# A spectral mixer's inverse table in two thirds, its load order, and the rings that its inverse tiles come from

## The chip, the cores and the metric

The kernel runs on one core of a Trainium2 chip. A core has a matrix engine (TensorE, "PE" in the profile, with its weight loads as "PEld"), VectorE ("DVE"), ScalarE ("ACT"), GpSimd ("POOL") and SyncE ("SP"), which here only issues DMAs. Work is passed between the engines by semaphores, and each engine runs its own instructions in order. PE writes to PSUM, eight banks of 2 KB in each of 128 partitions. The metric is the device time of one execution in microseconds. Before the change three runs gave 352.26, 358.77 and 361.63 us, with a median of 358.77.

## The reference

The forward pass mixes a sequence of 2048 rows with 448 features twice, once in the frequency domain and once by a two-layer network over the sequence; the outputs are the result and the gradients of everything.

```
h  = x + irfft2(rfft2(layernorm(x)) * (w_r + i w_i))        # 2048 x 448
u  = gelu(einsum("bsd,sf->bdf", layernorm(h), w1) + b1)      # f = 1792
out = h + transpose(einsum("bdf,fs->bds", u, w2) + b2)
grads of out with grad_out: x, w_r, w_i, w1, b1, w2, b2
```

## The kernel before

The Fourier transforms are matrix products with tables of cosines and sines that the host builds once (`_tables`). A transform over the 2048 rows is split 16 x 128, and the symmetries of a real input leave 225 of 448 columns; the sixteen parts of the row frequency are called j, and j and 16 − j are handled together.

The kernel is one long program. A scheduler puts the instructions of each engine in order, by the data they need; where the text says `issue_after`, an instruction is held behind another.

- **PSUM.** Eight banks in three rings: `m0` and `m1` with two buffers each (L215), and `sp` with four (L222). A tile that is asked for from a ring has to wait until the oldest buffer of that ring has been read.
- **Loads.** `nxt` (L237) chains the loads of SP in the written order. SP issues them in that order, and a load waits for the one eight places before it. Transposing loads go through `ld_t` (L232), others through `ld` (L226).
- **Forward transform.** `fft_rows` (L403) transforms rows in four quarters. `fft_cols` (L422) goes over eight pairs of j: two PSUM tiles from `sp`, a copy on ACT, sum and difference on VectorE (`gu`, `gv`, L484), then matmuls with the table `hf` into a tile of ring `m1` (L455), copied to `xs` by ACT.
- **Product.** `cmul` (L503) multiplies `xs` by the filter `w_t` in six groups of j, four VectorE operations each (L510 to L513), and writes over `w_t`.
- **Inverse transform.** `ifft_cols` (L519) takes the pairs of j in turn. `pair` asks for two tiles of PSUM (L522), one for each half of the partitions, and issues 16 matmuls of 64 x 128 (L534), whose moving operand is a row of the table `hi`. ACT copies the second tile (L551), and VectorE writes sum and difference of the two into `ab` (L553). The table `hi` holds for each j the pairs (cos, sin) and (−sin, cos), with the signs that the second half needs; it is 1 MB, `[128, 2, 16, 128]` in bf16 (L622).
- **Row steps.** Sixteen of them (L637): four matmuls with the table `di` (L578, L580), a copy on ACT, four with `kinv` (L587 to L590), then the residual and the layer norm. After every four steps ACT writes the normalized rows `hln` (L386).
- **Filling work.** `dg(j)` (L606) is 16 matmuls 448 wide of the gradient of the hidden layer (L610) with a transposed block of w2, `w2T`, into ring `m0`; after it the load of a further block is issued. dg(0) comes early; dg(1) to dg(3) and dg(4) to dg(13) are there to be put between the matmuls of the transforms. Behind them stand the first layer and the GELU (`gelu_in`, L683), the second layer (L752), and the gradient of the normalized rows (L811, with transposed blocks of w1, `w1T`).
- **Backward transform.** It uses the same functions with `twice=True`. There `fill(n)` hands out parts of the weight gradients (`gw2`, L259 for full chunks and L266 for tails), a counted number at each j; one part is half a block.

The loads around the change, and the three blocks behind them (L621 to L628 before):

```
load_w(w_t, nxt)
hi = consts.tile([P, 2, NJ, P], BF16, name="hi")
nxt(ld, hi[:], hnd["hi"].ap().rearrange("p (i j m) -> p i j m", i=2, j=NJ))
di0 = table([P, 4 * DF], "di0", "di")
kinv = table([P, 3, P], "kinv")
ident = table([P, P], "ident")
for j in range(1, 4):
    dg(j)
```

Of the kernel before, what the change touches and what calls it, by code (L numbers as in the profile page):

```python
# [11 lines left out]
BF16 = mybir.dt.bfloat16  # L12
F32 = mybir.dt.float32
ALU = mybir.AluOpType
# [3 lines left out]
P = 128  # L18
S = 2048
D = 448  # L20
DF = 225
# [4 lines left out]
NJ = 16  # L26
# [19 lines left out]
def _tables():  # L46
# [86 lines left out]
    p = 16 * (pp % 4) + pp // 4  # L133
# [15 lines left out]
            hf[64:, 3 + 2 * i + c] = sg * np.concatenate([np.sin(th), np.cos(th)], 1)  # L149
    tb["hf"] = _bf(hf.reshape(P, -1))  # L150

    hi = np.zeros((2, 64, 2, NJ, 2, 64))
    for c in range(2):
        for j in range(NJ):
            th = angle(j + 16 * c).T
            sg = -1.0 if c and j else 1.0
            hi[c, :, 0, j, 0], hi[c, :, 0, j, 1] = np.cos(th), sg * np.sin(th)
            hi[c, :, 1, j, 0], hi[c, :, 1, j, 1] = -np.sin(th), sg * np.cos(th)
    tb["hi"] = _bf(hi.reshape(P, -1))
    tb["ident"] = _bf(np.eye(P))  # L160
    return tb
# [3 lines left out]
def kernel(  # L165
# [29 lines left out]
    def slot(i, shape, name):  # L195
        return big.tile(shape, BF16, tag=f"s{i}", name=name)
# [18 lines left out]
    def ps_m(k, shape, dtype=F32):  # L215
        return psum.tile(shape, dtype, tag=f"m{k}", bufs=2, name=f"ps_m{k}")
# [5 lines left out]
    def ps_sp(shape, dtype=F32):  # L222
        return psum.tile(shape, dtype, tag="sp", bufs=4, name="ps_sp")
# [13 lines left out]
    def nxt(load, *args):  # L237
        if chain:
            with tc.issue_after(chain[-1].ins):
                chain.append(load(*args))  # L240
        else:
            chain.append(load(*args))
# [179 lines left out]
    def fft_cols(zt, dtab, dst, twice=False, fill=None):  # L422
        w = 226 if twice else DF

        def part(out, j, odd):
            lhs = [zt[:, 2 * odd + c, 2 * j:2 * j + 2, :] for c in range(2)]
            if twice:

                for c in range(2):
                    o = 113 * (2 * odd + c)  # L430
                    pe.matmul(out[:, 113 * c:113 * c + 113], lhsT=lhs[1 - c if odd else c], rhs=dtab[:, o:o + 113],
                              start=True, stop=True)
                return
            for c in range(2):
                o = DF * (2 * odd + c)
                pe.matmul(out, lhsT=lhs[c], rhs=dtab[:, o:o + DF], start=(c == 0), stop=(c == 1))

        def sums(nm):
            return k1([P, 2, w], nm)

        def in_order(t):
            return t.rearrange("p a (k c) -> p a c k", c=2) if twice else t

        def by_k(t):
            return t.rearrange("p a (c k) -> p a c k", c=2) if twice else t

        def out_j(j, u, v, behind):
            px = ps_sp([P, 2, DF]) if fill else ps_m(1, [P, 2, DF])
            if j:
                e = 1 + 2 * J_ORDER.index(j)  # L450
                lhs = [(b, g, hf[:, e + b, 64 * c:64 * c + 64]) for c in range(2) for b, g in ((1, v), (0, u))]
                for i, (b, g, m) in enumerate(lhs):

                    with tc.issue_after(behind[0].ins) if behind else nullcontext():
                        mm = pe.matmul(px[64 * b:64 * b + 64, i // 2, :], lhsT=m, rhs=g, start=True, stop=True)  # L455
                    behind = behind or [mm]
            else:
                for c in range(2):
                    for i, g in enumerate((u, v)):
                        pe.matmul(px[:, c, :], lhsT=hf[:, ((0, 2), (1, 0))[c][i], :], rhs=g,  # L460
                                  start=(i == 0), stop=(i == 1))
            ac.copy(out=dst[:, :, j * DF:(j + 1) * DF], in_=px[:])
            return behind

        def out_all(those):
            behind = []
            for args in those:
                behind = out_j(*args, behind)

        waiting = []
        for j in range(8):
            js = (j, 16 - j) if j else (0, 8)
            pt = [ps_sp([P, 2, w]) for odd in range(2)]
            for odd in range(2):
                for x, jj in enumerate(js):
                    part(pt[odd][:, x, :], jj, odd)
            first = 0 if j else 1
            gi = f2([P, 2, w], "gi")  # L480
            ac.copy(out=gi[:, first:, :], in_=pt[1][:, first:, :])  # L481
            u, v = sums("gu"), sums("gv")
            for g, op in ((u, ALU.subtract), (v, ALU.add)):
                ve.tensor_tensor(out=in_order(g[:, first:, :]), in0=by_k(pt[0][:, first:, :]),  # L484
                                 in1=by_k(gi[:, first:, :]), op=op)
            if not j:

                for g, ps in ((u, pt[0]), (v, pt[1])):
                    ac.copy(out=in_order(g[:, 0:1, :]), in_=by_k(ps[:, 0:1, :]))

            done = [(jj, u[:, x, 0:DF], v[:, 1 - x if j else x, 0:DF]) for x, jj in enumerate(js)]
            waiting += done
            if not fill or j:
                out_all(waiting[:-len(done)] if fill else waiting)
                waiting = done if fill else []
                if fill:
                    fill(2 if j in (1, 3, 6) else 1)
        out_all(waiting)


# [18 lines left out]
    def ifft_cols(ys, ab, twice=False, fill=None):  # L519
        def pair(js):  # L520

            pt = [ps_sp([P, 2, 2, P]) for b in range(2)]  # L522
            first = []
            for x, j in enumerate(js):
                for c in range(2):
                    for i in range(2):
                        for b in range(2):
                            d = slice(64 * b, 64 * b + 64)
                            jj = (16 - j) % 16 if b else j
                            k = jj * DF + (c if twice else 97 * c)  # L530
                            ks = slice(k, k + 2 * P - 1, 2) if twice else slice(k, k + P)

                            with tc.issue_after(first[-1].ins) if first else nullcontext():
                                mm = pe.matmul(pt[b][:, c, x, :], lhsT=ys[d, i, ks], rhs=hi[d, i, jj, :],  # L534
                                               start=(i == 0), stop=(i == 1))
                            first = first + [mm] if len(first) < 2 else first
            return pt

        def place(a, lo, hi_):
            return ab[:, a, :, :, lo:hi_, :].rearrange("p c h k l -> p k c h l")  # L540

        def view(t):
            return t.rearrange("p c x (k h l) -> p (x k) c h l", k=2, l=4)

        for j in (1, 2, 3, 4, 5, 6, 7, 0):
            pt = pair((j, 16 - j) if j else (8, 0))
            if fill and j:
                fill(1)
            n = 2 if j else 1
            t1 = f2([P, 2, 2, P], "t1")  # L550
            ac.copy(out=t1[:, :, 0:n, :], in_=pt[1][:, :, 0:n, :])  # L551
            for a, op in ((0, ALU.add), (1, ALU.subtract)):
                ve.tensor_tensor(out=place(a, 4 * j, 4 * j + 2 * n), in0=view(pt[0][:, :, 0:n, :]),  # L553
                                 in1=view(t1[:, :, 0:n, :]), op=op)
            if not j:
                for b in range(2):
                    ev(ab[:, :, :, :, 2 + b, :], view(pt[b][:, :, 1:2, :]), "av"[b])
# [48 lines left out]
    def dg(j):  # L606
        pg = ps_m(0, [P, D])
        with tc.issue_after(folded[min(j - 1, 3)][0].ins) if j else nullcontext():
            for t in range(NT):
                pe.matmul(pg[:], lhsT=w2T[j][:, t, :], rhs=go_nat[:, t, :], start=(t == 0), stop=(t == NT - 1))  # L610
        ev(du[:, j, 0:D], pg[:], "a")
        load_w2T()
# [6 lines left out]
        nxt(ld, hf[:, e0:e1], hf_d[:, e0:e1])  # L619
    w_t = slot(4, [P, 2, XW], "w_t")  # L620
    load_w(w_t, nxt)  # L621
    hi = consts.tile([P, 2, NJ, P], BF16, name="hi")  # L622
    nxt(ld, hi[:], hnd["hi"].ap().rearrange("p (i j m) -> p i j m", i=2, j=NJ))
    di0 = table([P, 4 * DF], "di0", "di")
    kinv = table([P, 3, P], "kinv")
    ident = table([P, P], "ident")
    for j in range(1, 4):
        dg(j)  # L628
    xs = slot(3, [P, 2, XW], "xs")
    fft_cols(zt, df1, xs)  # L630
    cmul(lambda r0, r1: (w_t[:, 0, r0 * DF:r1 * DF], w_t[:, 1, r0 * DF:r1 * DF]), xs, w_t, False)
    ab = slot(5, [P, 2, 2, NT, NR, 4], "ab")
    ifft_cols(w_t, ab)
    hn = x
# [197 lines left out]
            yield mm  # L832

    first = list(gw2(0, "aaaa"))
    fft_rows(dh, zt2, 3, "aava", first[-1], True)

    def blocks():
        for j in range(1, NFB):
# [6 lines left out]
    def fill(n):  # L845
        return [next(others) for i in range(n)]

    ds = slot(3, [P, 2, XW], "ds")
    fill(1)
    fft_cols(zt2, df0, ds, True, fill)  # L850
# [129 lines left out]
```

## Time and profile before

| | |
|---|---|
| three runs | 352.26, 358.77, 361.63 us |
| profiled execution | 351.85 us, its span 349.5 us |
| PE busy | 327.3 us (94%) |
| VectorE busy | 250.7 us (72%) |
| ACT busy | 207.6 us (59%) |
| granted PE clock | 1.00 |
| read from HBM, written | 32.41 MB, 28.93 MB |

The span is the time from the first to the last instruction; the profiled execution's own time has 2.35 us around it. Times in the rows of a timeline are in us from the span's start: first the start, then the duration, the engine, the line in the code, the operation, the output and the inputs. A bracket at the end of a row gives the idle time before it and what ended it. A matmul's duration runs from its first to its last element, so neighbouring matmuls overlap; the distance between two starts is what one costs. In a row of the windows stand the window, its length, then the busy time (and count) of PE, PEld, VectorE, ACT and POOL, the granted clock, the mean share of the DMA engines, and GB/s.

### The profile page before, as it was taken

How to read it: one execution, taken by the hardware profiler on the slowest of the kernel's cores; microseconds unless marked ns; L12 is line 12 of the kernel's file. 1: busy time of each engine (PE TensorE's matmuls, PEld its weight loads, DVE VectorE, ACT ScalarE, POOL GpSimd, SP SyncE). 2: the span in 40 equal slices, each digit the busy share in tenths (PEclk: the TensorE clock that was granted, in tenths of full speed). 3: DMA queues.
4: the chain of work that ended last, by engine and by line, in shares of the span. 5: the costliest groups of instructions: out<-in, count | busy, mean ns of one | idle time of the engine just before them, and what ended most of it. 6: DMA issues, size and time to landing. Idle time of an engine off the chain costs nothing.

```text
span 349.5 us, 6182 instructions
## 1 busy us (share of the span) xinstructions
PE 327.3 (94%) x2258; PEld 175.5 (50%) x2275; DVE 250.7 (72%) x586; ACT 207.6 (59%) x428; POOL 77.3 (22%) x133
## 2 busy tenths in 40 slices
PE   0799989999999999999999999999999999999995
PEld 0446544566655555555555555644544455454442
DVE  4894899777748988622225887864798797899932
ACT  3575643466759888200833444588885667777662
POOL 1000000011112110245511000001101124677960
PEclk9999999999999999999999999999999999999999
DMA  7999997999899999999999998999579437776485
GB/s 278 283 206 273 242 189 167 304 276 299 244 315 331 321 266 236 314 341 376 290 211 233 219 179 175 211 200 192 178 167 268 150 122 247 323 249 216 160 308 202
DMA packets 132878, 85.27 MB, mean 244 GB/s; under 512 B 92112, under 2 KB 124496, under 8 KB 132464
## 3 DMA queue, kind: packets, MB, share of 16 engines
q1 hardware_dynamic: 124400, 54.90, 68.2%
q0 software_dynamic: 8160, 29.85, 24.7%
q8 instruction: 18, 0.29, 0.4%
q14 instruction: 12, 0.10, 0.1%
q10 hardware_dynamic: 288, 0.13, 0.1%
HBM read 32.41 MB, written 28.93 MB: 175 GB/s over the span
## 4 chain that ended last, share of the span: by engine, by line
PE 62%; DVE 15%; DMA 9%; SPq 5%; issue 3%; ACT 3%; POOL 2%; DVEq 0%; ACTq 0%; POOLq 0%
PE ps_m L811 12%; PE ps_m L259 9%; PE ps_sp L752 6%; PE ps_m L752 6%; PE ps_m L683 6%; PE ps_sp L683 6%; PE ps_m L610 6%; DMA w_t<-in_A_w_i_dram 4%; DVE t_i L511 3%; DMA xs_b<-xs_d 3%; SPq L232 3%; DVE ab L553 2%; DVE t_r L510 2%; SPq L226 2%; DMA w2T<-in_B_w_dram 2%
## 5 line engine op out<-in xcount | busy, mean ns | idle before, releaser
L283 ACT CAST s<-ps_m 128x512 bf16<-128x512 f32 (+1 forms) x103 | 52.2, 573 | 15.9 <-PE ps_m L266 14.4
L610 PE MATMUL ps_m<-go_nat,w2T 128*128 128x448 bf16 x224 | 50.1, 359 | 1.6 <-DMA w2T<-in_B_w_dram 1.6
L811 PE MATMUL ps_m<-du,w1T 128*128 128x449 bf16 x224 | 43.4, 353 | 0.0
L259 PE MATMUL ps_m<-goT,g_t 128*128 128x512 bf16 x158 | 39.5, 380 | 0.7 <-issue 0.5
L229 POOL DMA_DIRECT2D out_dram<-s x28 | 15.2, 543 | 98.9 <-ACT s L283 77.7
L259 PE MATMUL ps_m<-du_t,hlnT 128*128 128x512 bf16 (+1 forms) x161 | 35.4, 352 | 1.2 <-ACT s L283 0.7
L752 PEld LDWEIGHTS <-w2c 128*128 128x128 bf16 x224 | 21.9, 98 | 20.5
L811 PEld LDWEIGHTS <-w1T 128*128 128x128 bf16 x224 | 21.7, 97 | 20.7
L683 PEld LDWEIGHTS <-w1c 128*128 128x128 bf16 x224 | 21.8, 98 | 20.5 <-issue 0.5
L610 PEld LDWEIGHTS <-w2T 128*128 128x128 bf16 x224 | 21.0, 99 | 18.6 <-DMA w2T<-in_B_w_dram 2.4
L752 PE MATMUL ps_sp<-gT,w2c 128*128 128x448 bf16 x112 | 30.3, 352 | 0.0
L752 PE MATMUL ps_m<-gT,w2c 128*128 128x448 bf16 x112 | 30.3, 352 | 0.0
L259 PEld LDWEIGHTS <-hlnT 128*128 128x128 bf16 x192 | 17.6, 98 | 21.1 <-issue 6.7
L757 DVE SCALAR_TENSOR_TENSOR h<-ps_m,b2col,hr 128x448 bf16<-128x448 f32 x8 | 5.1, 680 | 27.5 <-PE ps_m L752 27.5
L766 ACT ACTIVATE junk<-go_r 128x448 bf16<-128x448 bf16 x16 | 9.2, 577 | 24.4 <-DMA go_r<-in_grad_out_dram 23.9
L259 PEld LDWEIGHTS <-g_t 128*128 128x128 bf16 x168 | 14.6, 98 | 17.7 <-issue 3.8
L683 PE MATMUL ps_m<-hln,w1c 128*128 128x448 bf16 x112 | 23.0, 353 | 0.3 <-ACT hln L386 0.3
L683 PE MATMUL ps_sp<-hln,w1c 128*128 128x448 bf16 x112 | 22.7, 352 | 0.0
L775 ACT ACTIVATE nm<-ps_m,rstd_h 128x1 f32<-128x1 f32 x16 | 4.2, 262 | 29.7 <-PE ps_m L811 29.7
L553 DVE TENSOR_TENSOR ab<-ps_sp,t 128x512 bf16<-128x512 f32 (+1 forms) x32 | 19.2, 647 | 2.3 <-ACT t L551 2.3
L229 POOL DMA_DIRECT2D hn_d<-x x4 | 2.2, 548 | 78.1 <-DVE x L639 78.1
L484 DVE TENSOR_TENSOR gu<-ps_sp,gi 128x450 bf16<-128x450 f32 (+3 forms) x16 | 9.9, 619 | 12.7 <-ACT gi L481 12.7
(158 smaller groups left out, 647.5 us busy)
## 6 DMA issues: line engine op xcount, KB each, us to landing
w1c<-in_B_w_dram SPq DMA_DIRECT2D x7, 1024.0 KB, 10.5
w2c<-in_B_w_dram SPq DMA_DIRECT2D x8, 896.0 KB, 13.1
out_dram<-s POOLq DMA_DIRECT2D x14, 512.0 KB, 3.8
out_dram<-s POOLq DMA_DIRECT2D x14, 448.0 KB, 3.5
xs_d<-xs SPq DMA_DIRECT2D x1, 1800.0 KB, 7.5
xs_b<-xs_d SPq DMA_DIRECT2D x1, 1800.0 KB, 9.1
x<-in_A_x_dram SPq DMA_DIRECT2D x4, 448.0 KB, 4.3
go_nat<-in_grad_out_dram SPq DMA_DIRECT2D x2, 896.0 KB, 7.0
```

The lines of the kernel that those rows point to most:

```text
L229: return (eng or po).dma_start(out=out, in_=in_)
L232: return nc.sync.dma_start(out=out, in_=in_, transpose=True)
L259: last = pe.matmul(ps, lhsT=lhs[:, c, a], rhs=rhs[:, c, b], start=opens and c == 0, stop=not opens and c == 2)
L283: return ac.copy(out=out, in_=in_)
L484: ve.tensor_tensor(out=in_order(g[:, first:, :]), in0=by_k(pt[0][:, first:, :]), in1=by_k(gi[:, first:, :]), op=op)
L511: ve.tensor_tensor(out=t_i[:], in0=a[:, :, sl], in1=b[:, 1:2, sl].broadcast_to([P, 2, n]), op=ALU.mult)
L553: ve.tensor_tensor(out=place(a, 4 * j, 4 * j + 2 * n), in0=view(pt[0][:, :, 0:n, :]), in1=view(t1[:, :, 0:n, :]), op=op)
L610: pe.matmul(pg[:], lhsT=w2T[j][:, t, :], rhs=go_nat[:, t, :], start=(t == 0), stop=(t == NT - 1))
L683: pe.matmul(pu[:], lhsT=wc[:, h, o:o + P], rhs=hln[:, h, :], start=(h == 0), stop=(h == NT - 1))
L752: pe.matmul(p2[i][:], lhsT=w2c[t0 // 4][:, j, i * P:(i + 1) * P], rhs=gT[:, j, :], start=(j == 0), stop=(j == NFB - 1))
L766: ac.activation(out=junk[:], in_=go_r[:, h, :], func=ACT.Copy, accum_out=gb2[:, h:h + 1])
L811: w1_last = pe.matmul(pd[:], lhsT=w1T[:, j, :], rhs=du[:, j, 0:D + 1], start=(j == 0), stop=(j == NFB - 1))
```

## The change

Four things change.

1. The table `hi` that is loaded has two kinds and half the bytes (0.5 MB): (cos, sin), or (−sin, −cos) for the second half of the partitions with j not zero. It lies in places 1 and 2 of a tile with three places; place 0 is written on the chip as the negative of place 2, by one VectorE operation of 128 x 1024 behind the first group of `cmul`. The moving operand of the inverse matmul is now two places next to each other at one j: two runs of 64 elements, 1024 elements apart. This holds for the forward and the backward pass.
2. The loads of `di`, `kinv` and `ident` stand behind dg(1) to dg(3), and so behind the three w2T blocks that these ask for.
3. In the forward inverse transform the first tile of each pair comes from ring `m1` (two buffers), the second from `sp` (four). Backward both still come from `sp`.
4. Backward, the last quarter of the row transform stands behind one more part of the weight gradient, and the count at the second place where the column transform is filled is 1 where it was 2, so that the parts handed out are as many as before.

```diff
-    hi = np.zeros((2, 64, 2, NJ, 2, 64))
+    hi = np.zeros((2, 64, 2, NJ, 64))
     for c in range(2):
         for j in range(NJ):
             th = angle(j + 16 * c).T
-            sg = -1.0 if c and j else 1.0
-            hi[c, :, 0, j, 0], hi[c, :, 0, j, 1] = np.cos(th), sg * np.sin(th)
-            hi[c, :, 1, j, 0], hi[c, :, 1, j, 1] = -np.sin(th), sg * np.cos(th)
+            hi[c, :, 0, j], hi[c, :, 1, j] = (-np.sin(th), -np.cos(th)) if c and j else (np.cos(th), np.sin(th))
...
-                    fill(2 if j in (1, 3, 6) else 1)
+                    fill(2 if j in (3, 6) else 1)
...
-            pt = [ps_sp([P, 2, 2, P]) for b in range(2)]
+            pt = [ps_sp([P, 2, 2, P]) if fill else ps_m(1, [P, 2, 2, P]), ps_sp([P, 2, 2, P])]
...
+                            kind = i if b and jj else 1 - i
...
-                                mm = pe.matmul(pt[b][:, c, x, :], lhsT=ys[d, i, ks], rhs=hi[d, i, jj, :],
+                                mm = pe.matmul(pt[b][:, c, x, :], lhsT=ys[d, i, ks], rhs=hi[d, kind:kind + 2, jj, :],
                                                start=(i == 0), stop=(i == 1))
...
-    hi = consts.tile([P, 2, NJ, P], BF16, name="hi")
-    nxt(ld, hi[:], hnd["hi"].ap().rearrange("p (i j m) -> p i j m", i=2, j=NJ))
+    hi = consts.tile([P, 3, NJ, 64], BF16, name="hi")
+    nxt(ld, hi[:, 1:3], hnd["hi"].ap().rearrange("p (i j m) -> p i j m", i=2, j=NJ))
+    for j in range(1, 4):
+        dg(j)
     di0 = table([P, 4 * DF], "di0", "di")
     kinv = table([P, 3, P], "kinv")
     ident = table([P, P], "ident")
-    for j in range(1, 4):
-        dg(j)
     xs = slot(3, [P, 2, XW], "xs")
     fft_cols(zt, df1, xs)
-    cmul(lambda r0, r1: (w_t[:, 0, r0 * DF:r1 * DF], w_t[:, 1, r0 * DF:r1 * DF]), xs, w_t, False)
+
+    def neg_hi(r0, r1, last):
+        if r0 == 0:
+            with tc.issue_after(last.ins):
+                ve.tensor_scalar(out=hi[:, 0], in0=hi[:, 2], scalar1=-1.0, scalar2=None, op0=ALU.mult)
+
+    cmul(lambda r0, r1: (w_t[:, 0, r0 * DF:r1 * DF], w_t[:, 1, r0 * DF:r1 * DF]), xs, w_t, False, neg_hi)
...
     first = list(gw2(0, "aaaa"))
-    fft_rows(dh, zt2, 3, "aava", first[-1], True)
...
+    fft_rows(dh, zt2, 3, "aava", fill(1)[-1], True)
     ds = slot(3, [P, 2, XW], "ds")
     fill(1)
     fft_cols(zt2, df0, ds, True, fill)
```

In the rows of the changed kernel the lines of these functions have moved: L609 stands for L610, L533 for L534, L552 for L553, L577 and L579 for L578 and L580, L586 for L587, L688 for L683, L757 for L752, L816 for L811 and L415 for L417.

## Prediction

> **What bounds the kernel now.** I read the page's first and fourth part, then the waits of PE, then two views of the stretch where the change sits.
>
> ```profile
> span 349.5 us, 6182 instructions
> PE 327.3 (94%) x2258; PEld 175.5 (50%) x2275; DVE 250.7 (72%) x586; ACT 207.6 (59%) x428; POOL 77.3 (22%) x133
> PE 62%; DVE 15%; DMA 9%; SPq 5%; issue 3%; ACT 3%; POOL 2%; DVEq 0%; ACTq 0%; POOLq 0%
> ```
>
> PE is busy for 94% of the span, so a change that leaves the matmuls as they are can win only part of the other 22 us (349.5 − 327.3), or of the small gaps between groups of matmuls. The waits of PE between 9 and 110 us say where they are:
>
> ```profile
> PE ps_sp L417 <- DVE eo L411: 10.6, 1, 10.6
> PE ps_m L610 <- DMA w2T<-in_B_w_dram: 1.6, 2, 1.3
> PE ps_m L455 <- DVE gv L484: 0.8, 1, 0.8
> PE ps_m L683 <- ACT hln L386: 0.3, 1, 0.3
> PE ps_sp L534 <- DVE w_t L512: 0.2, 1, 0.2
> ```
>
> The 10.6 us are the start of the kernel, which the change leaves alone. The rest lies in the forward inverse transform. Two windows, the transform (40 to 65.5) and the sixteen row steps behind it (65.5 to 97):
>
> ```profile
> 40.00:65.50 25.50, 22.85 (x230) 11.75 (x228) 24.98 (x46) 11.29 (x23) 0.00 (x0) 1.00 0.95 222
> 65.50:97.00 31.50, 31.29 (x223) 21.45 (x224) 21.92 (x53) 19.91 (x37) 3.95 (x6) 1.00 1.01 260
> ```
>
> In the first PE is idle 2.65 us and VectorE only 0.52; in the second PE is the pace (0.21 idle). So the transform is tight on both engines, and whatever PE does there beyond its share is time won in the rows behind it.
>
> **The change part by part.**
>
> *The table and the order of the loads.* The queue of SP, and the landing of the one w2T block that PE waits for (the answer for that issue alone, then those of hi and ident):
>
> ```profile
> 28.07 0.58 SPq L226 DMA_DIRECT2D hi<-tab_hi  x1
> 28.70 0.44 SPq L226 DMA_DIRECT2D di<-tab_di  x1
> 32.01 0.32 SPq L226 DMA_DIRECT2D ident<-tab_ident  x1
> 34.12 25.02 SPq L232 DMA_TRANSPOSE w2T<-in_B_w_dram  x6
> ...
> DMA to landing us min/median/max: 13.2/13.2/13.2
> ...
> DMA to landing us min/median/max: 14.4/14.4/14.4
> ...
> DMA to landing us min/median/max: 11.6/11.6/11.6
> 47.34 1.12 PE L610 MATMUL ps_m<-go_nat,w2T 128*128 128x448 bf16 x5 [1.34 <-DMA w2T<-in_B_w_dram]
> 27.43 12.83 DMA w_t<-in_A_w_i_dram
> ```
>
> w_t's last part lands at 40.26 (27.43 + 12.83), hi at 42.5 (28.07 + 14.4), ident at 43.6 (32.01 + 11.6), w2T[5] at 47.3 (34.12 + 13.2): each follows the one before it. hi therefore takes some 2.25 us of the stream and w2T[5] 3.65. With hi at half its bytes and w2T[5] right behind it, hi lands at about 41.4 and w2T[5] at 41.4 + 3.65 = 45.0. Counting the matmuls in the new order, PE gets to this block at about 45.0. The wait of 1.34 goes; if the block is late by x, x stays, so the term is −1.34 to 0. The tables di, kinv and ident now land behind three w2T blocks, at 41.4 + 3 × 3.65 and their own 1.1, about 53.5: they are first read at 65.5, so this costs nothing unless they are 12 us later still. The issue of w2T[5] moves from 34.12 to about 28.7, past di, kinv and ident; w_t's transfers stand ahead of it in the queue and the landings above keep the order of issue, so I take VectorE's start (the first operation that reads the last of w_t, at 40.35) as unmoved.
>
> *The negation on VectorE.* One operation of 128x1024, bf16 to bf16 in SBUF, behind the first group of the complex product. No such shape is in the trace; the nearest:
>
> ```profile
> L689 DVE TENSOR_SCALAR zz<-zz 128x448 bf16<-128x448 bf16 x5 | 1.4, 272 | 0.7 <-ACT zz L687 0.7
> L731 DVE TENSOR_SCALAR du<-gb 128x14 bf16<-128x14 f32 x1 | 0.2, 198 | 0.0
> ```
>
> Not less than 0.27; at the price per element of the first row 272 × 1024/448 = 0.62; by a line through both rows 0.37 (0.17 ns an element). I take 0.4, nearer to the line because a fixed part plainly dominates. VectorE has no idle time to hide it in, so the whole of it moves the end of the transform. [...]
>
> *The matmuls' moving operand.* It becomes two runs of 64 elements where it was one of 128, in 256 matmuls. No row has two runs; the nearest is an operand read backwards (L588) beside one read forwards (L587):
>
> ```profile
> L587 PE MATMUL ps_sp<-eo,kinv x32: 257/257/270, 66.7 to 331.4; 128*128 128x225 bf16 x32
> L588 PE MATMUL ps_sp<-eo,kinv x32: 259/259/262, 66.8 to 331.5; 128*128 128x223 bf16 x32
> L534 PE MATMUL ps_sp<-hi,w_t x128: 212/216/228, 44.2 to 63.5; 64*128 64x128 bf16 x128
> ```
>
> An unusual walk costs 2 ns there; 0 is my value. At the other end each second run costs as much as the spread of the last row (16 ns): 4.1 us over 256.
>
> *Two rings and the order on PE.* What one switch between the two kinds of matmul costs:
>
> ```profile
> 59.09 0.23 PE L534 MATMUL ps_sp<-hi,w_t 64*128 64x128 bf16 x1
> 59.25 0.36 PE L610 MATMUL ps_m<-go_nat,w2T 128*128 128x448 bf16 x1
> ...
> 62.19 0.93 PE L610 MATMUL ps_m<-go_nat,w2T 128*128 128x448 bf16 x4
> 63.05 0.62 PE L534 MATMUL ps_sp<-hi,w_t 64*128 64x128 bf16 x15
> 63.60 1.88 PE L610 MATMUL ps_m<-go_nat,w2T 128*128 128x448 bf16 x9
> 65.52 0.36 PE L578 MATMUL ps_sp<-di,ab 128*128 128x225 bf16 x2
> ```
>
> One L534 alone holds PE from 59.09 to 59.25 (0.16), fifteen from 63.05 to 63.60 (0.55): 0.028 each and 0.13 for the switch. Four L610 take 0.86 from 62.19; in the row of nine they follow each other by (1.88 − 0.36)/8 = 0.19, so four are worth 0.76 and the way back costs 0.10. An interruption costs 0.22 in all. Before there are 14 groups of L534 in the transform, in the new order 9: 5 × 0.22 = −1.1. In the new order 76 of the 448-wide matmuls stand between the first L534 and the rows, where 61 stood: 15 more, or 15 × 0.19 = 2.85 us of work that the rows no longer have. Against this stand new waits. The first tile of each pair now comes from a ring of two that the forward transform uses until just before; a pair waits in it for both VectorE operations (L553) of the pair two earlier, and behind the waiting matmul stands every 448-wide one. Before, the same tile waited for the same pair, but finer groups hid it. Laying the new order on the durations above I find 0.7 us of such waits, the 0.4 of the negation among them (0.4 at least, 3.4 as a rival below). Rows begin at 65.5 + 2.85 − 1.34 − 1.1 + 0.7 = 66.6, with 2.85 us of their fillers done. VectorE's own chain allows 65.9, so a gain over 2.45 is excluded.
>
> The row steps keep their length: 92 filling matmuls become 91, but 14 more of them are the first matmuls of the next stage. Net: 1.1 − 2.85 = **−1.75**. The 0.3 us wait for hln behind the last row goes too, as 22 matmuls (4.2 us) that need nothing new stand there instead of 15 (2.8): **−0.3**.
>
> *Backward.* The last quarter of its row transform stands behind half a block of the weight gradient more (five matmuls, from 232.69 to 233.61 some 0.8 us where they stand now, second and third row).
>
> ```profile
> 231.78 1.07 PE L417 MATMUL ps_sp<-kf,e 128*128 128x128 bf16 x16 [0.49 <-DVE e L396]
> 232.69 0.38 PE L259 MATMUL ps_m<-goT,g_t 128*128 128x512 bf16 x1
> 233.00 0.61 PE L266 MATMUL ps_m<-goT,g_t 64*128 64x512 bf16 x4
> 233.84 0.99 PE L431 MATMUL ps_sp<-df,zt 128*128 128x113 bf16 x16 [0.23 <-ACT zt L283]
> ```
>
> They cover the 0.49 whole. The 0.23 stays covered only if the three row copies of zt, behind two more evacuations on ACT, are not later by more than the 0.5 that PE comes earlier; six full matmuls stand in between where one and four short ones stood. The one filler less at the second block pays this back in place and costs nothing unless VectorE's next sums are late (0 to 0.2). I take **−0.6** (−0.7 to 0).
>
> Sum: −1.75 − 0.3 − 0.6 = −2.65. The profiled execution took 351.85 us (span 349.5), so 349.2; the median of the three runs is 358.77, 1.02 times that, which gives **356.1**.
>
> **The rivals.**
>
> *The gain stops at the transposed w1.* Between 97 and 190 us the DMA engines never rest (below), and the stage that starts at 181.2 reads each block of w1T just after it lands (the row of the first of twelve blocks, and its landing):
>
> ```profile
> 97.00:190.00 93.00, 92.71 (x491) 47.78 (x489) 53.38 (x136) 51.42 (x108) 26.28 (x42) 1.00 1.15 299
> 181.20 5.53 PE L811 MATMUL ps_m<-du,w1T 128*128 128x449 bf16 x28
> 186.75 12.81 SPq L232 DMA_TRANSPOSE w1T<-in_B_w_dram  x6
> DMA to landing us min/median/max: 4.4/4.4/4.4
> ...
> 94.00:97.00 3.00, 3.00 (x23) 1.86 (x22) 1.64 (x5) 1.72 (x4) 0.76 (x1) 1.00 0.14 37
> 94.52 7.24 SPq L226 DMA_DIRECT2D w1c<-in_B_w_dram  x3
> ```
>
> The fifth block lands at 191.2 and is needed at 181.4 + 4 × 2.68 = 192.1, or 0.9 us later. If this stream does not come earlier, 2.05 of forward gain becomes 0.9, and the sum −1.5: 350.35, or 357.2. Against it: the stream is set going by the w1 blocks at 94.52, behind an idle stretch (share 0.14) that ends when the last 448-wide matmuls free a buffer, some 3.5 us earlier now, and one transposed w1 block moves ahead of two loads of w2.
>
> *Slower: the ring of two locks PE to VectorE.* If the seven pairs after the first each wait until VectorE has finished the pair two before, with no work ready behind them, PE runs at VectorE's pace: its last twelve L553 need 6.73 us, 1.12 a pair, where a pair and four 448-wide matmuls need 0.16 + 0.55 + 0.86. With 0.5 us lost at each of seven, 3.5 us, the forward part is −2.05 + 3.5 = +1.45 and the sum +0.85: 352.7, or 359.6. It decides from 2.65 us of waits beyond the 0.7. For it: VectorE is 98% busy there and gets 0.4 more. Against it: the depth in pairs is what it was, and in the row quoted first no wait for L553 is seen forward.
>
> *The moving operand's second run* costs up to 16 ns in each of 256 matmuls, 4.1 us in all: the sum +1.45, 353.3, or 360.3.
>
> *The clock.* In the first window PE is granted full clock (1.00) with a tenth of it idle, so gaps of that kind don't lower it. If longer waits on the ring did, from the first pair near 50 to the rows at 66, those 16 us would take up to twice as long: 349.2 + 16 = 365, or 372; at a quarter of that, 353 and 360. [...]
>
> *It does not do what it says*: w2T[5] is late all the same (+1.34) and the backward waits only move (+0.6). Sum −0.7: 351.15, or 358.0.
>
> **How the numbers follow.** A measurement of this kernel tells about 2%, 7.2 us, from no change; its three runs lie between 352.26 and 361.63. Chances: the forecast 0.5, the gain stopped 0.19, nothing of it 0.14, the ring 0.1, the second run 0.05, the clock 0.02. All but the last lie within 2% of 358.77. What leaves that band is the run itself, as the runs' own spread is −1.8% to +0.8% about the median; so faster 0.09, same 0.84, slower 0.07. The cases reach from 355.4 (VectorE's limit, −0.7 more) to 360.3; with the lowest of the runs shown less the gain below (352.3 − 2.7 = 349.6, and 1 for the unknown terms) the range is 348.5 to 361.
>
> **What would show it.** In the changed profile: no wait of L610 for w2T near 45; a tensor_scalar of about 0.4 us behind the first L512 and L513, after the last gv; fewer, longer groups of L533; row steps from about 66.6 with a last kinv matmul near 98, followed by no wait for hln; no wait of L415 for e near 230; the first w1T matmul near 179. L533 matmuls of more than 230 ns or waits of L533 for ab over 3 us would prove a rival, and a wait of L816 for w1T the first. I am wrong if VectorE starts later than 40.4, or if the waits in the transform grow by more than the fillers gained.

## The result, and the profile after

The changed kernel took 351.55 us (median of 22 runs, 348.27 to 358.21) and the kernel before, in its 22 runs, 354.35 us (351.32 to 361.63). Both have executions some 5 to 10 us longer than their lowest, which the ratio leaves out: it is 0.9896, with a 95% interval of 0.9863 to 0.9928. The change made the kernel 1.0% faster, 3.7 us (2.5 to 4.8) on the 351.85 of the profiled execution. A later set gave 0.9893 (0.9851 to 0.9936). That is within 2%, faster, and in the range given; the forecast was 2.65 us, or 0.75%. The time that was forecast, 356.1 us, is some 4.5 too high, because it hangs on the 358.77 of the first three runs; on the 354.35 of all 22 the same gain gives 351.7.

The first profile of the changed kernel (354.74 us, span 352.9) has a wait for a block of w2 that is looked at below. A second one (349.44 us, span 347.5) has none, and is compared here. Its page:

```profile
span 347.5 us, 6202 instructions
PE 327.1 (94%) x2275; PEld 175.2 (50%) x2275; DVE 250.3 (72%) x587; ACT 207.2 (60%) x428; POOL 76.6 (22%) x133
PE 70%; DVE 18%; ACT 7%; DMA 2%; issue 2%; ACTq 0%; DVEq 0%; POOLq 0%
```

PE does what it did (327.3 before) in 2.0 us less span. In the chain that ended last the share of DMA fell from 9% to 2%, and SP's 5% are gone. The waits of PE between 9 and 110 us (us in all, times, longest), and below them the windows of the transform and the row steps:

```profile
PE ps_sp L415 <- DVE eo L409: 11.2, 1, 11.2
PE ps_m L533 <- DVE ab L552: 1.4, 5, 0.5
...
PE ps_m L688 <- ACT hln L384: 0.3, 1, 0.3
...
PE ps_m L609 <- DMA w2T<-in_B_w_dram: 0.2, 1, 0.2
```

```profile
40.00:66.30 26.30, 24.89 (x254) 13.27 (x253) 25.27 (x47) 12.13 (x24) 0.00 (x0) 1.00 1.03 230
66.30:97.50 31.20, 31.01 (x224) 21.41 (x223) 21.84 (x53) 19.45 (x36) 3.96 (x6) 1.00 1.05 271
```

The wait for w2T is 0.2 where it was 1.6, and the 0.2 stand 13 us into the span, far ahead of w2T[5], the block on which PE waited 1.34 us before. In its place stands a wait of 1.4 us, in five pieces, for VectorE's sums `ab`: the ring of two. In the transform PE is busy 24.89 us instead of 22.85, in a window that is 0.8 longer; the row steps still run PE full. Rows of the timeline of the same profile, on the change's own instructions, and the answer for the line of the inverse matmuls (ns least/median/most):

```profile
45.09 0.42 DVE L634 TENSOR_SCALAR hi<-hi 128x1024 bf16<-128x1024 bf16 x1
66.36 0.36 PE L577 MATMUL ps_sp<-di,ab 128*128 128x225 bf16 x2
136.64 0.54 PE L757 MATMUL ps_m<-gT,w2c 128*128 128x448 bf16 x2
229.79 1.07 PE L415 MATMUL ps_sp<-kf,e 128*128 128x128 bf16 x16
```

```profile
L533 PE MATMUL ps_m<-hi,w_t x64: 212/216/228, 46.5 to 64.1; 64*128 64x128 bf16 x64
```

The negation takes 0.42 us. The matmul with two runs takes 216 ns, as with one. The row steps begin at 66.36, and the second layer at 136.64, where the timeline of the kernel before has 138.83. The row of L415 has no bracket: the wait for e of 0.49 is gone.

```profile
138.83 0.54 PE L752 MATMUL ps_m<-gT,w2c 128*128 128x448 bf16 x2
```

### The profile page after: what moved, and what is told of

It is laid out like the page before. It is cut to its first block, busy times and chain, and to the rows that moved or that the text cites. A ratio compares the mean times of both kernels' runs of the same rounds, so it can differ in the third digit from the quotient of the medians.

```text
span 352.9 us, 6185 instructions
## 1 busy us (share of the span) xinstructions
PE 328.2 (93%) x2258; PEld 175.9 (50%) x2275; DVE 249.3 (71%) x587; ACT 207.3 (59%) x428; POOL 78.3 (22%) x133
## 4 chain that ended last, share of the span: by engine, by line
PE 62%; DVE 13%; DMA 10%; SPq 8%; ACT 5%; issue 2%; ACTq 0%; DVEq 0%
PE ps_m L257 16%; PE ps_m L816 12%; DMA w2c<-in_B_w_dram 5%; SPq L230 5%; PE ps_m L609 5%; PE ps_m L688 4%; DMA w_t<-in_A_w_i_dram 4%; PE ps_sp L757 3%; PE ps_m L757 3%; PE ps_m L264 3%; SPq L224 3%; PE ps_sp L688 3%; DVE ab L552 3%; DVE t_i L509 2%; DVE t_r L508 2%
## 5 line engine op out<-in xcount | busy, mean ns | idle before, releaser
L609 PE MATMUL ps_m<-go_nat,w2T 128*128 128x448 bf16 x224 | 48.6, 357 | 0.0
L816 PE MATMUL ps_m<-du,w1T 128*128 128x449 bf16 x224 | 43.4, 353 | 0.0
L757 PEld LDWEIGHTS <-w2c 128*128 128x128 bf16 x224 | 22.6, 101 | 26.3 <-DMA w2c<-in_B_w_dram 3.9
L757 PE MATMUL ps_sp<-gT,w2c 128*128 128x448 bf16 x112 | 32.0, 369 | 3.5 <-DMA w2c<-in_B_w_dram 3.5
L816 PEld LDWEIGHTS <-w1T 128*128 128x128 bf16 x224 | 21.7, 97 | 20.7
L757 PE MATMUL ps_m<-gT,w2c 128*128 128x448 bf16 x112 | 32.0, 369 | 0.0
L688 PEld LDWEIGHTS <-w1c 128*128 128x128 bf16 x224 | 21.8, 98 | 20.2 <-issue 0.5
L609 PEld LDWEIGHTS <-w2T 128*128 128x128 bf16 x224 | 21.0, 98 | 16.8 <-issue 1.2
L688 PE MATMUL ps_m<-hln,w1c 128*128 128x448 bf16 x112 | 23.1, 352 | 0.3 <-ACT hln L384 0.3
L688 PE MATMUL ps_sp<-hln,w1c 128*128 128x448 bf16 x112 | 22.7, 352 | 0.0
L281 ACT CAST zt<-ps_sp 128x512 bf16<-128x512 f32 x26 | 13.5, 598 | 5.4 <-PE ps_sp L415 5.4
```

Of the source, the lines that this page charges most:

```text
L281: return ac.copy(out=out, in_=in_)
L688: pe.matmul(pu[:], lhsT=wc[:, h, o:o + P], rhs=hln[:, h, :], start=(h == 0), stop=(h == NT - 1))
L757: pe.matmul(p2[i][:], lhsT=w2c[t0 // 4][:, j, i * P:(i + 1) * P], rhs=gT[:, j, :], start=(j == 0), stop=(j == NFB - 1))
L816: w1_last = pe.matmul(pd[:], lhsT=w1T[:, j, :], rhs=du[:, j, 0:D + 1], start=(j == 0), stop=(j == NFB - 1))
```

## The experiments

### The forward parts, undone one at a time

How soon VectorE can start on the last part of w_t differs from run to run: its first such operation (t_i) starts between 9.3 and 11.8 us after the first matmul of the column transform, with no link to the order of loads. So forward gains are read from the start of t_i to the first matmul of the second layer (w2c), in one profiled execution of each kernel, by rows like these of the kernel with both tiles from `sp`:

```profile
40.44 0.86 DVE L509 TENSOR_TENSOR t_i<-xs,w_t 128x1350 bf16<-128x1350 bf16 x1 [1.06 <-DMA w_t<-in_A_w_i_dram]
65.94 0.36 PE L577 MATMUL ps_sp<-di,ab 128*128 128x225 bf16 x2
137.93 0.54 PE L757 MATMUL ps_m<-gT,w2c 128*128 128x448 bf16 x2
```

| kernel | t_i to rows | rows to w2c | t_i to w2c |
|---|---|---|---|
| before; backward part alone | 25.17; 25.17 | 73.31; 73.31 | 98.48; 98.48 |
| changed, first profile | 26.19 | 70.29 | 96.48 |
| loads alone | 25.16 | 72.18 | 97.34 |
| changed, both tiles from sp | 25.50 | 71.99 | 97.49 |
| changed, loads as before | 26.19 | 70.77 | 96.96 |
| changed, full table | 25.99 | 70.90 | 96.89 |

Two later kernels with the changed forward part gave 96.46 and 96.46. (In the second profile VectorE started so early, 9.33 us in, that the rows began 36.0 us after the first column matmul, as in two others, and it was not the limit: 96.96 there.)

**Both tiles from sp again:**

```diff
-            pt = [ps_sp([P, 2, 2, P]) if fill else ps_m(1, [P, 2, 2, P]), ps_sp([P, 2, 2, P])]
+            pt = [ps_sp([P, 2, 2, P]) for b in range(2)]
```

> The changed kernel with both tiles of a forward inverse pair from the ring of four again; table, load order, negation and the backward part stay. The order on PE goes back to 12 groups of the 64-row matmuls in the transform (9 with the two rings). Theory A: the two rings are worth the switches less the new waits on them, 3 x 0.22 - 0.7, so about 0: ratio 0.990 to 0.992, and no wait for ab in the forward part. Rival (the rings are where the gain is): ratio 0.995 or more.

The time from t_i to w2c is 1.0 us longer than with two rings. Without the second ring the rows begin 0.7 earlier, but 69 of the 448-wide matmuls stand ahead of them where 76 stand with two, and the row steps take 1.7 longer. The listed waits for ab are gone, as expected; that the rings are worth about nothing was wrong. One pair of j shows where the 1.0 comes from, first in this kernel, then in the first profile of the changed one:

```profile
59.58 0.23 PE L533 MATMUL ps_sp<-hi,w_t 64*128 64x128 bf16 x1
59.74 0.36 PE L609 MATMUL ps_m<-go_nat,w2T 128*128 128x448 bf16 x1
60.07 0.60 PE L533 MATMUL ps_sp<-hi,w_t 64*128 64x128 bf16 x15
60.61 0.55 PE L609 MATMUL ps_m<-go_nat,w2T 128*128 128x448 bf16 x2
```

```profile
60.92 0.23 PE L533 MATMUL ps_m<-hi,w_t 64*128 64x128 bf16 x1 [0.28 <-DVE ab L552]
60.92 0.23 PE L533 MATMUL ps_sp<-hi,w_t 64*128 64x128 bf16 x1
...
61.47 1.12 PE L609 MATMUL ps_m<-go_nat,w2T 128*128 128x448 bf16 x5
```

With one ring the first matmul of the pair stands alone (0.16 us, to 59.74) and fifteen follow later (0.54). With two rings all sixteen, eight into each tile, stand together and take 0.55. Added up from start to start with the waits left out, the 128 matmuls of the inverse hold PE for 5.50 us before, 5.64 in this kernel and 4.62 with two rings. The 448-wide ones of the hidden layer's gradient, 151 from 2.0 us behind t_i to the second layer in each, hold it for 31.4, 31.2 and 30.8, as PE comes back to them less often. So the rings save 1.4 us by three groups fewer (12 to 9) and add 0.4 us of waits.

The ratio, 0.9958 (0.9918 to 0.9999), meets the rival's 0.995. But it rests on four of the twelve executions (350.16 to 352.44), the other eight take 357.6 us and more, and the profiled one of these waits for DMA (below). So the size is read from the profile.

**Loads as before, full table, loads alone:**

```diff
-    for j in range(1, 4):
-        dg(j)
     di0 = table([P, 4 * DF], "di0", "di")
     kinv = table([P, 3, P], "kinv")
     ident = table([P, P], "ident")
+    for j in range(1, 4):
+        dg(j)
```

> The changed kernel with di, kinv and ident loaded ahead of the w2T blocks again. Theory A: w2T[5] is issued near 34 and lands near 46.2, PE waits 1.2 to 1.5 for it, and the first matmul of the second layer comes at 137.9 instead of 136.6. Rival (with the halved table the order doesn't matter): 136.6 to 136.9.

> The changed kernel with the full 1 MB table and so without the negation; order of loads, rings and backward part as changed. Theory A: w2T[5] lands at 45.6 instead of 44.5 and PE, which wants it at 44.7, waits 0.9; VectorE is 0.4 ahead; the first matmul of the second layer at 136.9 to 137.3, where the changed kernel has 136.6. Rival (the half megabyte is worth less than the negation costs): 136.3 or earlier.

The full table is the kernel without `neg_hi`, with the table and the moving operand of before. "Loads alone" is the kernel before with only the opposite of the diff above.

> The kernel before with the order of loads of the change alone (three w2T blocks ahead of di, kinv and ident; full table, both tiles from sp). Theory A: w2T[5] lands 1.1 us later than in the changed kernel (44.5), at 45.6, where PE wants it near 45.1: a wait of 0.5 in place of 1.34, and the first matmul of the second layer at 138.0 instead of 138.8. Rival (the order of loads is worth nothing without the halved table): 138.6 or later.

One row each, in that order, of PE's wait for w2T[5]:

```profile
47.42 0.55 PE L609 MATMUL ps_m<-go_nat,w2T 128*128 128x448 bf16 x2 [0.73 <-DMA w2T<-in_B_w_dram]
```

```profile
45.44 0.74 PE L610 MATMUL ps_m<-go_nat,w2T 128*128 128x448 bf16 x3 [0.74 <-DMA w2T<-in_B_w_dram]
```

```profile
47.40 0.74 PE L610 MATMUL ps_m<-go_nat,w2T 128*128 128x448 bf16 x3 [0.73 <-DMA w2T<-in_B_w_dram]
```

Each of the two edits alone halves the wait of 1.34, and both together end it. Counted from the landing of the last part of w_t, the block lands 7.0 us later before, 5.6 to 5.8 with one of the edits, and 4.5 and 4.4 with both. Undoing the loads costs 0.5 us, undoing the table 0.4 at most, negation saved included; the loads alone give 1.1. Their gains overlap: the second one mends what the first left. By the absolute times (138.83, 136.78 and 139.05 at w2c) the first expectation is missed by 0.9 and the third falls to its rival (138.6 or later); t_i started at 41.87 and 41.71 there, and the times from t_i are not touched by that.

### The backward part alone

```diff
-    fft_rows(dh, zt2, 3, "aava", first[-1], True)
...
+    fft_rows(dh, zt2, 3, "aava", fill(1)[-1], True)
...
-                    fill(2 if j in (1, 3, 6) else 1)
+                    fill(2 if j in (3, 6) else 1)
```

> The kernel before with the backward part of the change alone (the last quarter of the row transform behind one more part of the weight gradient, the count of parts 1 instead of 2 at one place). Its forward order is that of the kernel before. Theory A: the first matmul of the second layer stays at 138.8; from the last w1T matmul to the last goT matmul it takes 65.4 us instead of 65.96, so -0.5 to -0.6, and no wait for e near 230. Rival: the waits only move to the next quarter or to the column transform: 65.9.

The forward part repeats that of before to 0.01 us (98.48), though w2c comes at 139.88, as t_i started at 41.40. From the last w1T matmul to the last goT matmul it took 65.45 us, and 65.96 before: −0.51. Every profile with the backward part has 65.45 to 65.47, and all without it 65.96 or 65.97. The timeline of that profile around 240 us:

```profile
240.43 1.07 PE L417 MATMUL ps_sp<-kf,e 128*128 128x128 bf16 x16
241.34 1.46 PE L259 MATMUL ps_m<-goT,g_t 128*128 128x512 bf16 x6
242.92 0.99 PE L431 MATMUL ps_sp<-df,zt 128*128 128x113 bf16 x16
```

No row has a bracket, which is printed from 0.15 us on. The wait for e is gone. That for zt has shrunk from 0.23 to 0.12 (242.80, the end of the second row, to 242.92), and a new one of 0.06 us stands in the column transform. So theory A holds, with a small part of the waits left.

### The negation, twice

```diff
+                ve.tensor_scalar(out=hi[:, 0], in0=hi[:, 1], scalar1=-1.0, scalar2=None, op0=ALU.mult)
                 ve.tensor_scalar(out=hi[:, 0], in0=hi[:, 2], scalar1=-1.0, scalar2=None, op0=ALU.mult)
```

> The changed kernel with the negation of 128x1024 written twice (first from the other place of the table, then as before); PE's order is the same. What sets the first row step? Counted from the first matmul of the column transform (30.35 in the second profile of the changed kernel) the row steps begin 36.0 later and the second layer 106.3 later. Theory C (VectorE's chain sets it, PE fills the time up to it): both 0.4 us later, 36.4 and 106.7. Rival (PE sets it, as the prediction's sum has it, and VectorE has room): 36.0 to 36.1 and 106.3.

VectorE in its timeline:

```profile
45.36 0.42 DVE L634 TENSOR_SCALAR hi<-hi 128x1024 bf16<-128x1024 bf16 x1
45.69 0.62 DVE L508 TENSOR_TENSOR t_r<-xs,w_t 128x900 bf16<-128x900 bf16 x1
46.23 0.42 DVE L635 TENSOR_SCALAR hi<-hi 128x1024 bf16<-128x1024 bf16 x1
```

The rows began 36.43 us after the first column matmul, as theory C has it, but t_i started 0.7 later than in the profile that the expectation was made from. From t_i it is 26.41, 0.22 more than the 26.19 of the other profiles with the changed order; w2c comes 96.50 after t_i, where it was 96.46 to 96.48. So half of the second negation shows at the rows and nothing of it at the second layer. The order on PE was not quite the same either. This doesn't settle which engine sets the rows; with 26.19 in four profiles in which VectorE started late and 36.0 from the column transform in three in which it started early, both limits lie close together.

### Why executions of one kernel differ by 10 us

The first profile of the changed kernel: its wait at the second layer in the timeline, and the windows around it (the last three numbers of a window are the granted clock, the DMA share and GB/s):

```profile
161.77 0.93 PE L757 MATMUL ps_sp<-gT,w2c 128*128 128x448 bf16 x2 [3.47 <-DMA w2c<-in_B_w_dram]
```

```profile
139.00:158.00 19.00, 19.00 (x103) 9.79 (x100) 7.65 (x21) 1.51 (x3) 6.03 (x10) 1.00 1.12 296
162.00:166.00 4.00, 4.00 (x12) 1.62 (x11) 0.00 (x0) 0.00 (x0) 3.96 (x7) 0.50 1.15 326
166.00:170.00 4.00, 4.00 (x18) 1.80 (x16) 0.00 (x0) 0.00 (x0) 1.18 (x2) 0.78 1.04 409
170.00:181.00 11.00, 11.00 (x60) 5.68 (x58) 2.46 (x4) 9.79 (x29) 2.20 (x4) 1.00 1.16 251
```

PE waits 3.5 us; when it goes on, its clock is at half (0.50), and full again (1.00) some 6 us later. The second layer takes 48.97 us there and 42.37 in the second profile: 6.6 us lost, 3.5 of them as the wait and 3.1 by the clock. In the changed order the first w1T block is loaded ahead of w2, which it was not before. The next kernel puts that back (w2_mid is the fourth load of w2; the lines that name it are left out):

```diff
-        with tc.issue_after(chain[-1].ins):
+        with tc.issue_after(w2_mid.ins):
             w1T_last = ld_t(w1T[:], w1Tv[h])
```

> The changed kernel with its transposed w1 blocks held behind the first four loads of w2, as they stood before the change. In the first profile of the changed kernel the sixth load of w2 lands at 161.7 and is needed at 157.8; in the kernel before it landed at 152.1 and was needed at 160.0. Theory A: the sixth load lands near 154, no wait for w2, ratio 0.990 with no execution over 352. Rival B: the wait stays within 1 us of 3.5, since w2 is late because of the DMA engines' load and not of the order.

Its timeline, and its windows:

```profile
190.44 6.34 SPq L230 DMA_TRANSPOSE w1T<-in_B_w_dram  x3
195.60 10.70 PE L818 MATMUL ps_m<-du,w1T 128*128 128x449 bf16 x44 [5.83 <-DMA w1T<-in_B_w_dram]
```

```profile
189.00:196.00 7.00, 1.17 (x6) 0.37 (x5) 3.88 (x9) 0.98 (x2) 0.00 (x0) 0.79 1.12 225
196.00:199.00 3.00, 3.00 (x10) 1.20 (x9) 0.00 (x0) 0.00 (x0) 0.00 (x0) 0.50 1.18 218
203.00:226.00 23.00, 23.00 (x141) 12.37 (x139) 18.79 (x47) 9.67 (x21) 0.00 (x0) 1.00 0.87 178
```

No wait for w2, as theory A has it, though the second profile of the changed kernel has none either, so the order is not shown to be the cause. But now PE waits 5.8 us for the fifth w1T block, which is issued at 190.4, behind the transposed loads of the forward activations and of grad_out. The same wait stands in the profiles of the kernels with both tiles from sp (5.7 us), the backward part alone (4.9), the loads alone (4.2) and the full table (7.1), each in an execution of 358.8 to 359.9 us; with the loads as before it is 1.5 us, the clock stays at 1.00, and the execution takes 352.2. Ratio 0.9968 (0.9913 to 1.0024), single executions 349.6 to 359.2, where theory A had 0.990 and none over 352: the order of w2 alone mends nothing.

All transposed w1 blocks behind six loads of w2 (the same diff with the sixth load):

> The changed kernel with all transposed w1 blocks held behind the first six loads of w2. Theory A: the sixth load lands some 15 us before its use, PE never waits for w2, ratio 0.990 (0.988 to 0.992), and single executions stay within 1% of each other. Rival B: as the changed kernel, single executions from 348 to 358. A third way: the w1 blocks now come too late for the stage that starts near 179 and PE waits there instead, ratio 0.995 or more.

Ratio 0.9894 (0.9844 to 0.9943), five of six executions from 348.5 to 349.7, one of 354.4, so not all within the 1% of theory A. In the profile w2 is early by 20 us and PE waits 0.5 us for w1T. The changed kernel itself, on the same chip, had six executions from 348.1 to 350.5:

> The changed kernel again, for a second profile. In its first profile the forward part is 2.26 us ahead at the first matmul of the second layer (136.57 against 138.83), and then PE waits 3.5 us there for a block of w2 and runs at a mean granted clock of 0.92. Theory A (the gain is made in the forward transform and in the backward row transform, and the wait for w2 is an accident of the load order that only some executions pay): here the wait is under 1 us, the gradient of the normalized rows starts near 178.9, the span is near 346.3 and the ratio to the kernel before 0.990. Rival B (the wait for w2 is always there, and the gain comes from elsewhere, behind it): the wait of 3 to 4 us stands in this profile too, with a ratio of 0.990.

Theory A holds in this profile: no wait for w2, the w1T stage from 179.0, and a ratio of 0.9893. The span is 347.5 where 346.3 was expected.

Then the transposed load of grad_out in four pieces, behind w1 blocks 4, 6, 8 and 10, on both kernels (with six loads of w2 first):

```diff
-        if h == 4:
-            goT = slot(2, [P, 4, S], "goT")
-            with tc.issue_after(w1T_last.ins):
-                ld_t4(goT[:], grad_out[0])
+        if h == 5:
+            goT = slot(2, [P, 4, S], "goT")
+        if h in (5, 7, 9, 11):
+            c = (h - 5) // 2
+            o = min(128 * c, 320)
+            with tc.issue_after(w1T_last.ins):
+                ld_t(goT[:, c, :], grad_out[0][:, o:o + 128])
...
```

> The changed kernel with six loads of w2 ahead of the first transposed w1 blocks, and with the transposed load of grad_out cut into four that stand behind the w1 blocks 4, 6, 8 and 10 instead of ahead of block 4. In the profiles in which PE waits for w1T, block 4 is issued at 189 to 193, behind grad_out, though its buffer is free near 184. Theory W (the order of the loads is what makes executions differ): block 4 issued near 184 and landed before 190, no wait for w1T or w2, every execution within 1% of the lowest, median near 349.3. Rival (the DMA engines are full, whatever the order): a wait for a later w1 block instead, and executions of 353 and more remain.

> The kernel before with the same two moves of loads (w2 ahead of w1T, grad_out in four). Theory W: every execution within 1% of the lowest, median near 351.8, and the changed kernel with these loads is 2.2 to 3.2 us faster than this one: what the matmul work gained, without waits for DMA. Rival: executions of 355 and more remain, ratio 0.997 to 1.003 against the kernel before.

The changed kernel with these loads: SP in the timeline, then PE's wait for w1T and the window of the stage.

```profile
183.16 1.64 SPq L230 DMA_TRANSPOSE w1T<-in_B_w_dram  x1
184.86 2.67 SPq L230 DMA_TRANSPOSE goT<-in_grad_out_dram  x1
187.62 4.25 SPq L230 DMA_TRANSPOSE w1T<-in_B_w_dram  x2
```

```profile
PE ps_m L821 <- DMA w1T<-in_B_w_dram: 3.2, 3, 1.5
```

```profile
180.00:226.00 46.00, 42.83 (x245) 22.11 (x244) 33.45 (x80) 16.69 (x34) 2.82 (x6) 1.00 1.00 197
```

Block 4 is issued at 183.2 and no longer late. But sixteen transposed loads don't fit in the stage (DMA share 1.00 from 180 to 226 us), and PE waits three times for later blocks, 0.7 to 1.5 us each, with the clock at 1.00. Ten executions of the changed kernel lie between 352.25 and 355.41, ten of the kernel before between 353.88 and 356.62: the long executions are gone, and the short ones too. Ratios to the kernel before are 1.0058 (1.0031 to 1.0084) and 1.0075 (1.0038 to 1.0111). Between the two medians lie 1.1 us, where I expected 2.2 to 3.2. The stage is paced by DMA in both (PE waits 3.2 us for w1T in each), so that a gain ahead of it may be lost in it; but their VectorE also started 11.8 and 9.3 us in, so this is no clean measure.

At last only the second half of the plain load of grad_out (0.9 MB) behind block 5, with its sums:

```diff
+        if h == 6:
+            with tc.issue_after(w1T_last.ins):
+                ld(go_r[:, 8:16, :], rows(grad_out[0])[:, 8:16, :])
+        if h >= 8:
+            sum_go(h)
...
```

> The changed kernel with six loads of w2 ahead of the first transposed w1 blocks, and with the second half of the plain load of grad_out (0.9 MB, read from row step 8 of that stage on) behind w1 block 5 instead of ahead of the transposed loads; the sums over that half move with it on ACT. Cutting the transposed load of grad_out in four took 2.4 us of the stream for each piece and made PE wait 3.2 us in three places; this half is some 3 us in all, against 12 blocks of 2.4 in 33 us. Theory W (PE waits for w1T because too many bytes stand ahead of block 4): block 4 lands 3 us earlier than needed, no wait of more than 0.5 us for w1T or w2, executions within 1% of each other and a median near 349.3, 2 to 3 us under that of the kernel before at its lowest. Rival (another transfer takes the room): waits of 2 us and more for a later block, median 351 or more.

Ratio 0.9951 (0.991 to 0.9991), executions from 348.45 to 354.35, with a median of 350.87; the kernel before reached 357.94 on the same chip, and the changed kernel 358.21 in its first set but only 350.48 in its second. The profiled one waits 0.8 us for w1T. Neither expectation is met: theory W had 0.5 us at most and all executions within 1%, the rival 2 us and more. No version here is clearly better than the changed kernel.

## Why the prediction was right

**Direction and range** were right; the size was 2.65 us against 3.7 (2.5 to 4.8). Of its terms:

- *w2T[5]* was put at 45.0 and PE's need at 45.0. It landed at 44.5 and 43.4 in the two profiles; PE came to it at 44.7 and 44.8. The term of 1.34 holds, in the first profile by 0.2 us; behind hi the block took 3.2 and 3.1 of the stream, not 3.65.
- *The negation* was put at 0.4 and took 0.42, 0.05 over the line through the two nearest rows (0.37).
- *The two runs* cost nothing: 216 ns, as in the row of L534 before.
- *The two rings* were the term that was mis-sized, in both of its parts. Five switches saved less the waits, −1.1 + 0.7, made −0.4, and the expectation for the kernel without them said about 0; they are worth 1.0. The waits are 1.4, not 0.7. The timeline of before has 13 groups of L534 in the transform, not 14, so four switches went and not five. And the price of 0.22, read at one lone matmul, was too low: by the sums in the experiment on the rings, 5.50 to 4.62 and 31.4 to 30.8, with 0.07 in the neighbouring matmuls, the four are worth 1.55, or 0.39 each. That 76 of the 448-wide matmuls stand ahead of the rows, where 61 did, gains nothing by itself, as the row steps have as many fewer. (The 76 are counted from the place where the first L534 stood before; 67 of them stand behind the first one now.)
- *Rows at 66.6*: 66.28 and 66.36. At a like start of VectorE, the rows come 1.0 later than before and the second layer 2.0 earlier. The forecast had 1.1 and, with the wait for hln, 2.05.
- *The wait of 0.3 for hln* was to go. It is still 0.29 in both profiles of the changed kernel: 15 matmuls stand between the last kinv matmul and the wait, as before, and not the 22 of the forecast, and ACT wrote hln only at 100.6 to 100.7. This step failed.
- *Backward*, −0.6: it is −0.51, and so in all profiles; 0.12 us of the wait for zt stayed. The five matmuls that cover the waits, put at some 0.8, take 0.92 by the rows of before.

The mechanisms of the sum are there, but that its forward total fits so well, 2.05 against 2.0, is luck. It had −1.34 − 1.1 + 0.7 − 0.3. Measured are −1.34 for w2T, −1.55 for the groups, +1.25 for the waits for ab (1.37, less 0.11 that stood there before), 0 for hln, and −0.35 of small waits that the sum did not have, 0.21 of them for w_t.

So 2.0 and 0.5 are shown, 2.5 us in all. That the two like profiles differ by 2.41 (351.85 to 349.44) is no check of it. Their spans differ by 2.1: the column transform begins 0.7 later, from there to the second layer it takes 2.9 less, the backward part 0.5 less, and what stands behind the last goT matmul 0.6 more. The rest up to the ratio's 3.7 is not settled; the lowest executions of the two kernels lie 3.05 and 3.14 apart in the two sets. VectorE started 1.3 us sooner after the column transform in the second profile than in that of before, without a cause that the orders show; and short waits for w1T, such as the 1.5 us above, may be in the executions of the kernel before that the ratio keeps. Both are only argued.

*The rivals.* That the gain would stop at the transposed w1 was priced at 1.1 us. Its mechanism is real: the saturated stream (DMA share 1.12 in the 7 us of the wait with w2 as before) and the block read just after it lands. It did not stand in either profile of the changed kernel. In five profiles of other kernels, one of them with the forward part of before, it costs 4.2 to 7.1 us, and some 2 more by the clock in the two of them where that was read (0.50 for a little over 4 us), and the fastest executions of two of them (349.6 and 350.2) seem to be spared. I took the one profile's margin of 0.9 us as fixed, and it moves by some 6 us between executions. The clock came down, to 0.50, the half that the rival on the clock reckoned with, though not from the ring, as that rival had it: waits of 0.2 to 0.5 us at the ring left it at 1.00. The rival on the slower side (the ring locks PE to VectorE) would have shown more than 2.65 us of waits beyond 0.7; it was 1.4 in all.

## What to carry to other kernels

Price an order by adding up, from start to start, what each kind of matmul holds the fullest engine for, and the waits beside it: the price of a switch read at one place came out at little more than half. Two edits that feed the same wait share its price, so undo them one at a time before adding them up. And where the DMA engines are full (a share of 1.15 between 97 and 190 us before the change), one profile's margin of a microsecond is no margin: look at several executions before a load is put behind others.

## What was not expected of the hardware

Behind waits of 3.5 us (the first profile of the changed kernel), 5.8 us (w2 as before) and 4.9 us (the backward part alone) PE goes on at half the granted clock, 0.50, for some 4 to 6 us: the first two in the windows above, the third from 198 to 202 us. The executions with the other three such waits, of 4.2, 5.7 and 7.1 us, have mean clocks of 0.99, 0.99 and 0.984, where those of the later profiles without such a wait have 0.999 or 1.000. After a wait of 1.5 us, with the loads as before, the clock stayed at 1.00, by that kernel's timeline and window:

```profile
193.59 6.69 PE L816 MATMUL ps_m<-du,w1T 128*128 128x449 bf16 x34 [1.50 <-DMA w1T<-in_B_w_dram]
```

```profile
188.00:196.00 8.00, 6.50 (x35) 3.14 (x34) 5.95 (x14) 1.97 (x4) 0.00 (x0) 1.00 1.03 201
```

Between 1.9 us, the longest wait for w1T in the kernel of before with grad_out in four (mean clock 1.000), and 3.5 us no profile has a wait, so from what length on the clock comes down is not shown, nor what sets the time back to full clock. The wait of 10.6 us ahead of the first matmul, before the change, stands apart: the recorded clock is 1.00 behind it, though sixteen matmuls of 128x128 take 1.89 us there and 1.07 later.

The transposed load of the forward activations, issued at 154.9, landed at 180.0 in the kernel with w2 as before, and in the second profile of the changed kernel it took from 155.9 to 173.9. So the same load behind the same loads, in nearly the same order, took 25.1 us and 18.0. That goes with the wait for w1T in the one and none in the other, but it does not decide it alone: with the loads as before the load took 25.7 us (154.75 to 180.45), and PE waited 1.5 us only, in a stage that began 2.3 us later. Where the spread comes from stays open.
